# A second inner seven-product scheme in the last matrix product of a fused attention and MLP kernel, with VectorE and TensorE held in program order

## The chip, the cores and the metric

The kernel runs on one core of a Trainium2 chip. The metric is the device time of one execution in microseconds (us); lower is better. Times are medians of several executions. The profiled execution of each kernel was one of them. "Span" is the time from the first to the last instruction of a profiled execution.

## The reference, cut to what matters

```python
def _B_ref(x, w1, b1, w2, b2):
    h = _layernorm(x, axis=-1)
    u = jnp.einsum("bsd,sf->bdf", h, w1) + b1      # "mixer 1"
    u = _gelu(u)
    y = jnp.einsum("bdf,fs->bds", u, w2) + b2      # "mixer 2": the change is here
    return y.transpose(0, 2, 1)

h = x + _A_ref(_layernorm(x), A_wqkv, A_wo)        # linear attention, not touched
h2 = h + _B_ref(_layernorm(h), B_w1, B_b1, B_w2, B_b2)
```

Here S = 2048, D = 1024 and F = 3584. Mixer 2 multiplies w2 (transposed, 2048 x 3584) by the GELU output (3584 x 1024), and adds b2 and the residual h.

Of the kernel before, what the change touches and what calls it, by code (L numbers as in the profile page):

```python
# [8 lines left out]
P = 128  # L9
# [18 lines left out]
def kernel(  # L28
# [170 lines left out]

    class Inner:  # L200
# [7 lines left out]
        def sums(self):  # L208
            sm = [pools["is"].tile([P, self.nk, P], FP16, tag=self.tag, bufs=4, name="is")[:] for _ in range(4)]
            nc.vector.tensor_tensor(sm[0], self.a21, self.a22, ALU.add)  # L210
            nc.vector.tensor_tensor(sm[1], sm[0], self.a11, ALU.subtract)
            nc.vector.tensor_tensor(sm[2], self.a11, self.a21, ALU.subtract)
            nc.vector.tensor_tensor(sm[3], self.a12, sm[1], ALU.subtract)
            self.lhs.update({5: sm[0], 6: sm[1], 7: sm[2], 3: sm[3]})

        def mm(self, m, ps, start):
            for k in range(self.nk):
                nc.tensor.matmul(  # L218
                    ps, lhsT=self.lhs[m][:, k, :], rhs=self.mov[m][:, k, :],
                    start=(start and k == 0), stop=(k == self.nk - 1), skip_group_check=True,  # L220
                )
# [33 lines left out]
    class Product7:  # L255
# [9 lines left out]
        def prefetch(self):  # L265
            pass

        def asum(self, m):
            a, b, op = {
                5: (self.a21, self.a22, ALU.add),  # L270
                6: (self.lhs.get(5), self.a11, ALU.subtract),
                7: (self.a11, self.a21, ALU.subtract),
                3: (self.a12, self.lhs.get(6), ALU.subtract),
            }[m]
            t = pools["sa"].tile([P, self.nk, P], FP16, tag="sa", name="sa")[:]
            self.lhs[m] = t
            return nc.vector.tensor_tensor(t, a, b, op)  # L277
# [4 lines left out]
        def mm(self, m, ps, start, ks=None, cols=slice(0, CW)):  # L282
            lhs, mv = self.lhs[m], self.mov[m]
            for k in range(self.nk) if ks is None else ks:
                nc.tensor.matmul(  # L285
                    ps[:, cols],
                    lhsT=lhs[:, k, :],
                    rhs=mv(k)[:, cols],
                    start=(start and k == 0),
                    stop=(k == self.nk - 1),  # L290
                    skip_group_check=True,
                )
# [55 lines left out]
    class Mixer1(Product7):  # L348
# [11 lines left out]
        def evac_shared(self, fh, ps):  # L360
            t = cpool.tile([P, BANK], F32, tag=f"t{fh}", name="t1")
            nc.vector.tensor_tensor(t[:], ps[:], self.e[:], ALU.add)
            self.evac(fh, 1, t)
# [5 lines left out]
    class Mixer2(Product7):  # L369
        def __init__(self, p):  # L370
            super().__init__(p, w2_tiles[p], NFP, gmov)

        def prefetch(self):
            self.hr = {}
            for sh in range(2):
                for dh in range(2):
                    t = outp.tile([P, CW], BF16, tag=f"hr{self.p % 2}{sh}{dh}", bufs=2 if (sh, dh) == (1, 0) else 1, name="hr")
                    nc.sync.dma_start(t[:], h_dram[2 * self.p + sh][:, dh * CW:(dh + 1) * CW])
                    self.hr[sh, dh] = t

        def out(self, sh, dh, a, b, op):
            i = 2 * self.p + sh
            ot = outp.tile([P, CW], BF16, tag="ot", bufs=3, name="ot")
            op(ot[:, a:b], b2_sb[:, i:i + 1])
            nc.sync.dma_start(o_dram[i * P:(i + 1) * P, dh * CW + a:dh * CW + b], ot[:, a:b])

        def evac(self, sh, dh, ps, a=0, b=CW):
            self.out(sh, dh, a, b, lambda ot, bias: nc.vector.scalar_tensor_tensor(
                ot, ps[:, a:b], bias, self.hr[sh, dh][:, a:b], ALU.add, ALU.add))

        def evac_shared(self, sh, ps):
            t = cpool.tile([P, BANK], F32, tag=f"t{sh}", name="t2")

            def op(ot, bias):
                nc.vector.scalar_tensor_tensor(t[:], ps[:], bias, self.e[:], ALU.add, ALU.add)
                nc.vector.tensor_tensor(ot, t[:], self.hr[sh, 1][:], ALU.add)

            self.out(sh, 1, 0, CW, op)
# [7 lines left out]
    class Quad:  # L406
# [12 lines left out]
        def sum1(self, m, h, ps, es):  # L419
            A, B, c = self.sts[m].A, self.sts[m].B, self.cols(h)  # L420
            nc.vector.tensor_tensor(A[:, c], ps, es, ALU.add)
            nc.scalar.copy(B[:, c], A[:, c])
# [4 lines left out]
        def sum5(self, m, h, ps, es):  # L427
            nc.vector.tensor_tensor(self.sts[m].e[:, self.cols(h)], ps, es, ALU.add)
# [11 lines left out]
        def prefetch(self):  # L440
            for st in self.sts:
                st.prefetch()

        def run(self, pend, nxt, on_p4=nop, before_p7=nop, on_p7=nop, cut=None):
            nk = self.sts[0].nk

            def interleave(n, fs):
                steps = [(f, k) for f in fs for k in range(nk)]
                t = len(steps)
                cuts = [0, (5 * t + 8) // 16, (9 * t + 8) // 16, (12 * t + 8) // 16, t]  # L450

                def fill(q):
                    part = steps[cuts[q]:cuts[q + 1]]
                    for f in fs:
                        ks = [k for g, k in part if g is f]
                        if ks:
                            f(ks)

                for f in (n.i1, 0, n.i6, n.i2, 1, n.i5, n.i7, 2, n.i3, 3, n.i4):
                    fill(f) if isinstance(f, int) else f()  # L460

# [725 lines left out]
    cpool = ctx.enter_context(tc.tile_pool(name="cpool", bufs=1))  # L1187
    assert NFP % 2 == 0 and NSP % 2 == 0 and NSP >= 4 and NFP >= 6
    inner1 = mctx.enter_context(tc.tile_pool(name="inner1", bufs=1, side="right"))
    pools["is"] = inner1  # L1190
# [29 lines left out]
    pools["sa"] = ctx.enter_context(tc.tile_pool(name="sapool2", bufs=6, side="right", reuse_waits="tile"))  # L1220
# [4 lines left out]
    pools["is"] = inner2  # L1225
# [11 lines left out]
    def derived(m, of):  # L1237
        def make():
            ts = [g2pool.tile([P, H2, CW], FP16, tag=f"gs{h}", name=f"gs{h}") for h in range(2)]
            for h, sl in enumerate(spans):  # L1240
                nc.vector.tensor_tensor(ts[h][:], *of(sl), ALU.subtract)
# [3 lines left out]
    make_t3 = derived(7, lambda sl: (gT2[:, sl, :], gE[:, sl, 0:CW]))  # L1245
    make_t4 = derived(4, lambda sl: (gO[:, sl, 0:CW], gT2[:, sl, :]))
    load_w2(1, wpool)
    for p in (2, 3):
        load_w2(p, w2b)
    mov5, sums5 = inner_moving(gE[:, :, CW:D], NFP, inner2, "gi5")  # L1250

    def quad2(u):
        return Quad([Mixer2(2 * u), Mixer2(2 * u + 1)], None, mov5)
# [11 lines left out]
    for st in pend:  # L1265
        st.prefetch()
        if st is pend[1]:
            for m in (5, 6, 7, 3):
                st.asum(m)
            make_t3()  # L1270
# [3 lines left out]
        st.p6()  # L1274
    sums5()
    nxt.pre(5)
# [3 lines left out]
    nxt.pre(6)  # L1280
    nxt.pre(7)
    for st in pend:
        st.p3()
    nxt.pre(3)
    for u in range(1, NSP // 2):
        cur = nxt
        cur.prefetch()
        last = 2 * u + 2 == NSP
        pend, nxt = cur.run(
            pend, lambda: None if last else quad2(u + 1),  # L1290
            on_p4=after_p4(u), on_p7=make_t4, cut=CW - P if last else None,
# [33 lines left out]
```

## The kernel before: what the change touches

Mixer 2 works on eight products p = 0 to 7. One product gives 256 output rows by all 1024 columns. In a matmul, the stationary operand is the one that the code passes as `lhsT`, the moving one is `rhs`; the result goes to PSUM, the memory in which matmuls add up. A product is split into 2 x 2 blocks (row tile, even or odd tile of F, half of the columns), and instead of eight block products the kernel does seven (the Strassen-Winograd scheme): M1 to M7. Each is 14 matmuls of 512 columns. The stationary sums S5, S6, S7, S3 are made by VectorE from the weights of that p, the moving sums T2, T3, T4 from the GELU output (T3 and T4 share one pair of buffers, "gs", so they are made anew all the time).

Products 2 to 7 run as three pairs, called quads. Over the two products of a pair, one M is itself again a 2 x 2 block product. "Inner" does it with seven products of 7 matmuls of 256 columns, 49 in all, in place of 28 of 512 columns. Before, this was done for M5 only:

```python
        def i7(self):                                  # class Inner
            self.mm(7, self.c, False)
            self.sink_sum(1, 1, self.c, self.es[:])    # VectorE adds from PSUM
        def i3(self):
            self.mm(3, self.b, False)                  # b and c: two halves of one PSUM tile
            self.sink_sum(0, 1, self.b, self.es[:])
...
            if self.mov1 is not None:                  # Quad.run; mov1 is None in mixer 2
                ...
            else:
                for st in self.sts:
                    st.p1()                            # M1, plain: 14 matmuls of 512 each
                for st in pend:
                    st.p4()                            # M4 of the pair before
            on_p4()                                    # T3; loads of the next weights
            nxt = nxt()
            ...
            interleave(self.in5, [st.p6 for st in self.sts])   # M5 inner, between it M6
            pre(5)                                     # S5 of the next pair
            for st in self.sts:
                st.p2()
            ...
```

An eviction takes a finished result out of PSUM. That of M2 or M4 was one VectorE operation (PSUM + bias + residual). The order of the instructions on each engine is chosen by the scheduler of the kernel language, except where `tc.keep_in_program_order` ("pin") ties an instruction behind the one written before it.

## Time and profile before

| | before |
|---|---|
| device time, median of 3 (lowest to highest) | 575.07 us (575.03 to 575.7) |
| span of the profiled execution | 573.1 us |
| TensorE (PE) busy | 566.0 us, 99% |
| VectorE (DVE) / ScalarE (ACT) busy | 67% / 44% |
| mixer 2, first to last matmul | 402.88 to 570.2 us |

The head of the profile page gives the span, each engine's busy time and, in its section on the chain that ended last, the share of each engine in that chain.

```profile
span 573.1 us, 8081 instructions
...
PE 566.0 (99%) x3061; PEld 287.2 (50%) x3061; DVE 383.8 (67%) x731; ACT 254.7 (44%) x547; POOL 1.8 (0%) x8
...
PE 93%; DVE 3%; DMA 2%; ACT 2%; issue 1%; SPq 0%; ACTq 0%
```

Busy time by stretch, before. The columns are the stretch, its length, the busy time of PE, PEld (weight loads), DVE, ACT and POOL with their number of instructions, then the granted clock of TensorE (1.00 is full), the DMA share and GB/s. The first row is all of mixer 2, the other two are whole quads.

```profile
402.88:570.20 167.32, 167.32 (x862) 83.63 (x860) 113.94 (x119) 16.73 (x35) 0.00 (x0) 1.00 0.44 119
480.75:522.36 41.61, 41.61 (x219) 21.20 (x217) 27.52 (x32) 4.11 (x9) 0.00 (x0) 1.00 0.51 139
522.36:563.97 41.61, 41.61 (x219) 21.24 (x218) 22.36 (x25) 4.36 (x10) 0.00 (x0) 1.00 0.12 39
```

TensorE is busy in 167.32 of 167.32 us at full clock: nothing is left to hide a saving in, and nothing to gain but TensorE work. VectorE is busy for two thirds of a quad.

The timeline of TensorE, before, at the start of a quad (start, length, engine, line, operation, count). The end of a matmul is modelled, so read from start to start.

```profile
480.75 3.18 PE L285 MATMUL psA_5063<-gE,wq 128*128 128x512 f16 x14
483.77 3.19 PE L285 MATMUL psA_5080<-gE,wq 128*128 128x512 f16 x14
486.79 1.67 PE L285 MATMUL psC_4858<-gs_4997,wq 128*128 128x512 f16 x7
```

The two M1 products take 486.79 - 480.75 = 6.04 us. Seven matmuls of 256 columns are read in the same way at the M5 inner product, where two such blocks stand next to each other:

```profile
456.97 0.93 PE L218 MATMUL psI_4818<-gE,is 128*128 128x256 f16 x7
457.74 0.93 PE L218 MATMUL psI_4819<-gi_4452,is 128*128 128x256 f16 x7
458.50 1.24 PE L285 MATMUL psB_4758<-gT_4434,sa 128*128 128x512 f16 x5
```

One takes (458.50 - 456.97) / 2 = 0.765 us.

The chain that ended last, before, its last pieces:

```profile
569.43 0.80 PE psC_5618 L285 x14
570.22 0.02 issue
570.25 0.35 DVE ot L388
```

After the last matmul there is one VectorE operation and then the output transfer, until 573.1 us.

### The profile page before, as it was taken

The page shows a single profiled execution, that of the slowest core. Times are in us where ns is not written, and L with a number is a line of the kernel's source. Part 1 is how long each engine was busy: PE and PEld are TensorE (multiplying, and loading weights), DVE is VectorE, ACT ScalarE, POOL GpSimd, SP SyncE. Part 2 cuts the span into 40 slices and gives each one's busy share as a digit, 9 for nine tenths or more (in the row PEclk, how much of TensorE's full clock was granted, in tenths as well). Part 3 has the DMA queues.
Part 4 walks back from the last instruction along what each step waited for, and adds up shares of the span by engine and source line. Part 5 has one row for each costly group of instructions (what it writes and reads, how often), then busy time and mean ns, then how long its engine had stood idle before and what let it go on. Part 6 is the DMA issues. An engine that isn't in the chain of part 4 may idle for free.

```text
span 573.1 us, 8081 instructions
## 1 busy us (share of the span) xinstructions
PE 566.0 (99%) x3061; PEld 287.2 (50%) x3061; DVE 383.8 (67%) x731; ACT 254.7 (44%) x547; POOL 1.8 (0%) x8
## 2 busy tenths in 40 slices
PE   8999999999999999999999999999999999999997
PEld 3444444455555444446555565564444554544544
DVE  6898887556767879863745727442989558557535
ACT  5657777656667776445445354463110100100100
POOL 1000000000000000000000000000000000000000
PEclk9999999999999999999999999999999999999999
DMA  9934432039536762104041240425971852842001
GB/s 309 352 74 83 85 73 38 19 113 318 104 73 130 184 174 102 55 2 146 1 148 55 93 148 1 148 75 146 233 189 47 218 140 67 218 120 73 19 27 47
DMA packets 97798, 66.59 MB, mean 116 GB/s; under 512 B 32082, under 2 KB 91744, under 8 KB 97760
## 3 DMA queue, kind: packets, MB, share of 16 engines
q1 hardware_dynamic: 97024, 65.42, 41.7%
q10 hardware_dynamic: 672, 0.66, 0.3%
q8 instruction: 24, 0.39, 0.3%
q14 instruction: 14, 0.11, 0.1%
q0 software_dynamic: 64, 0.01, 0.0%
HBM read 50.34 MB, written 8.39 MB: 102 GB/s over the span
## 4 chain that ended last, share of the span: by engine, by line
PE 93%; DVE 3%; DMA 2%; ACT 2%; issue 1%; SPq 0%; ACTq 0%
PE acc_t L964 9%; PE acc_t L1112 9%; PE psB L695 4%; PE psC L695 4%; PE psA L695 4%; PE psE L695 2%; PE nd_ps L1063 1%; DMA xr<-in_A_x_dram 1%; PE psB_4758 L285 1%; PE psC_5500 L285 1%; PE psC_5181 L285 1%; PE psB_5064 L285 1%; PE psC_4858 L285 1%; PE psA_4757 L285 1%; PE psC_4527 L285 1%; PE psB_4550 L285 1%
## 5 line engine op out<-in xcount | busy, mean ns | idle before, releaser
L285 PEld LDWEIGHTS <-sa 128*128 128x128 f16 x716 | 70.0, 98 | 77.3 <-issue 0.7
L285 PEld LDWEIGHTS <-wq 128*128 128x128 bf16 x590 | 57.1, 98 | 61.7 <-issue 1.0
L964 PE MATMUL acc_t<-xnT,wq_sb 128*128 128x512 bf16 x256 | 58.0, 379 | 0.0
L1112 PE MATMUL acc_t<-wo_sb,pqT 128*128 128x512 bf16 x256 | 56.1, 379 | 0.0
L277 DVE TENSOR_TENSOR sa<-wq 128x1024 f16<-128x1024 bf16 (+1 forms) x44 | 36.4, 830 | 6.9 <-DMA wq<-in_B_w_dram 2.8
L1112 PEld LDWEIGHTS <-pqT 128*128 128x128 bf16 x256 | 24.8, 98 | 29.0
L964 PEld LDWEIGHTS <-wq_sb 128*128 128x128 bf16 x256 | 24.5, 98 | 27.4
L166 ACT ACTIVATE e_sb<-acc_t 128x512 bf16<-128x512 f32 x40 | 23.9, 597 | 26.5 <-PE acc_t L964 24.3
L170 DVE TENSOR_SCALAR e_sb<-e_sb 128x512 bf16<-128x512 bf16 x64 | 18.5, 289 | 25.4 <-ACT e_sb L166 24.8
L218 PEld LDWEIGHTS <-is 128*128 128x128 f16 x276 | 26.9, 98 | 14.3 <-issue 3.0
L695 PEld LDWEIGHTS <-xs 128*128 128x128 f16 x208 | 20.0, 98 | 23.3 <-DVE xs L681 1.3
L695 PE MATMUL psA<-wkv,xnT 128*128 128x512 bf16 x104 | 26.7, 379 | 0.0
L1123 DVE BATCH_NORM_STATS2 hst<-acc_t 128x6 f32<-128x512 f32 x32 | 22.1, 693 | 6.7 <-ACT h_bf L1122 6.5
L1110 ACT CAST acc_t<-xr 128x512 f32<-128x512 bf16 x32 | 19.0, 593 | 13.4 <-DVE hst L1123 13.3
L695 PEld LDWEIGHTS <-xnT 128*128 128x128 bf16 x156 | 15.3, 98 | 18.5 <-issue 0.2
L167 ACT ACTIVATE r_sb<-acc_t 128x512 bf16<-128x512 f32 x40 | 23.7, 593 | 0.0
L619 PE MATMUL acc_t<-wkv,xnT 128*128 128x512 bf16 x96 | 21.6, 379 | 0.7 <-ACT xnT L872 0.7
L1084 DVE TENSOR_TENSOR o_sb<-nd_ps,rd 128x384 bf16<-128x384 f32 (+1 forms) x48 | 21.7, 504 | 0.6 <-ACT rd L1079 0.4
L588 DVE BATCH_NORM_STATS2 st<-x_sb 128x6 f32<-128x512 bf16 x32 | 20.5, 681 | 1.6 <-DMA x_sb<-in_A_x_dram 1.6
L277 DVE TENSOR_TENSOR sa<-sa,wq 128x1024 f16<-128x1024 f16 (+1 forms) x22 | 18.3, 831 | 3.9 <-PE psC_4858 L285 2.3
L277 DVE TENSOR_TENSOR sa<-wq,sa 128x1024 f16<-128x1024 bf16 (+1 forms) x22 | 18.3, 831 | 3.7 <-PE psI_5141 L218 1.1
L1122 ACT CAST h_bf<-acc_t 128x512 bf16<-128x512 f32 x32 | 18.4, 575 | 1.0 <-PE acc_t L1112 0.9
(722 smaller groups left out, 979.1 us busy)
## 6 DMA issues: line engine op xcount, KB each, us to landing
wq<-in_B_w_dram SPq DMA_DIRECT2D x14, 1024.0 KB, 7.7
wq<-in_B_w_dram SPq DMA_DIRECT2D x8, 1792.0 KB, 10.0
xr<-in_A_x_dram SPq DMA_DIRECT2D x16, 256.0 KB, 3.1
out_dram<-ot SPq DMA_DIRECT2D x31, 128.0 KB, 1.7
x_sb<-in_A_x_dram SPq DMA_DIRECT2D x15, 256.0 KB, 3.2
wkv<-in_A_wqkv_dram SPq DMA_DIRECT2D x2, 1024.0 KB, 9.5
wq_sb<-in_A_wqkv_dram SPq DMA_DIRECT2D x2, 1024.0 KB, 12.7
wo_sb<-in_A_wo_dram SPq DMA_DIRECT2D x2, 1024.0 KB, 6.4
```

The source lines that it names most:

```text
L166: pin(nc.scalar.activation(e_sb[:], src, ACT.Exp))
L167: pin(nc.scalar.activation(r_sb[:], src, ACT.Relu))
L218: nc.tensor.matmul(ps, lhsT=self.lhs[m][:, k, :], rhs=self.mov[m][:, k, :], start=(start and k == 0), stop=(k == self.nk - 1), skip_group_ ...
L277: return nc.vector.tensor_tensor(t, a, b, op)
L285: nc.tensor.matmul(ps[:, cols], lhsT=lhs[:, k, :], rhs=mv(k)[:, cols], start=(start and k == 0), stop=(k == self.nk - 1), skip_group_check ...
L588: return nc.vector.bn_stats(st[:, c, :], x_sb[:, c * CW:(c + 1) * CW])
L619: mm = nc.tensor.matmul(pp[:, 0:CW], lhsT=xnT[:, kt, i * P:(i + 1) * P], rhs=wkv[:, kt, c * CW:(c + 1) * CW], start=(kt == 0), stop=(kt == ...
L695: pin(nc.tensor.matmul(ps[:], lhsT=lhs[:, k, :], rhs=rhs[:, k, :], start=(start and k == 0), stop=(k == hk2 - 1), skip_group_check=True,))
L964: nc.tensor.matmul(qp[:, 0:SW], lhsT=wq_sb[:, kt, j * P:(j + 1) * P], rhs=xnT[:, kt, u * SW:(u + 1) * SW], start=(kt == 0), stop=(kt == ND ...
L1084: nc.vector.tensor_tensor(o_sb[:, b * JPB * P:(b * JPB + nsl) * P].rearrange("p (s h e) -> p s h e", h=HB, e=DH), blk[:, :, 0:P].rearrange ...
L1112: nc.tensor.matmul(ap_[:, 0:CW], lhsT=pqT[:, j, i * P:(i + 1) * P], rhs=wo_sb[:, j, dc * CW:(dc + 1) * CW], start=(j == 0 and not SEED_RES ...
L1123: nc.vector.bn_stats(st[:, dc, :], ap_[:, 0:CW])
```

## The change

Its intent: do M1 of the three quads by the inner scheme as well, and so save the columns of 7 matmuls of 256 per quad (49 x 256 in place of 28 x 512). The rest makes room for that: sums for the M1 inner product, evictions of M2 and M4 split into a ScalarE part (PSUM + bias) and a light bf16 add on VectorE, the same light add as the second sum in an eviction of M3 or M7, S7 written over the weights that it is made from, four instead of six sum buffers, and the instructions of VectorE and TensorE held in the order in which they are written (`Held`). "S6 sums behind those of M5" is the order of the two lines after `st.begin()`. The diff, cut to its core:

```diff
+    class Held:
+        on = False
+        ...
+        def __getattr__(self, name):
+            op = getattr(self.engine, name)
+            return (lambda *a, **kw: pin(op(*a, **kw))) if Held.on else op
+
+    dve, pe = Held(nc.vector), Held(nc.tensor)
     ... (sums, matmuls and evictions of both mixers call dve and pe)
     class Mixer2(Product7):
+        def asum(self, m):
+            if m != 7:
+                return super().asum(m)
+            t = self.a21.bitcast(FP16)           # S7 in place
+            self.lhs[7] = t
+            return dve.tensor_tensor(t, self.a11, self.a21, ALU.subtract)
     ...
         def out(self, sh, dh, a, b, op):
             ...
             op(ot[:, a:b], b2_sb[:, i:i + 1])
+            dve.tensor_tensor(ot[:, a:b], ot[:, a:b], self.hr[sh, dh][:, a:b], ALU.add)
     ...
         def evac(self, sh, dh, ps, a=0, b=CW):
-            self.out(sh, dh, a, b, lambda ot, bias: nc.vector.scalar_tensor_tensor(
-                ot, ps[:, a:b], bias, self.hr[sh, dh][:, a:b], ALU.add, ALU.add))
+            self.out(sh, dh, a, b, lambda ot, bias: nc.scalar.activation(
+                ot, ps[:, a:b], ACT.Identity, bias=bias, scale=1.0))
     ...
+        def begin2(self):
+            self.asums(5)
+            self.in1 = self.inner(1)             # four inner sums of M1
+
+        def run2(self, pend, nxt, on_p4, on_p7, cut):
+            sts = self.sts
+            for st in sts:
+                st.begin()
+            in5 = self.inner(5)                  # inner sums of M5
+            self.asums(6)                        # S6 behind them
+            self.interleave(self.in1, [st.p4 for st in pend])
+            on_p4()                              # T3, weight loads
+            ...
+            self.asums(7)
+            self.interleave(in5, [st.p6 for st in sts])
+            self.asums(3)
+            nxt = nxt()
+            for st in sts:
+                st.p2()
+            ...
+            if nxt is not None:
+                nxt.begin2()
+            for st in sts:
+                st.p7(cut if st is sts[-1] else None)
+            on_p7()                              # T4
+            for st in sts:
+                st.p3()
+            return sts, nxt
     ...
+    def less_b11(t, sl):                         # T3 is mended, as the M1 inner sums
+        ...                                      # overwrite a part of the GELU output
     ...
+    sums1()                                      # moving sums of the M1 inner product
     sums5()
     ...
+    Held.on = True
     for u in range(1, NSP // 2):
     ...
-        pend, nxt = cur.run(
+        pend, nxt = cur.run2(
```

More of the change, by code (lines that the diff above doesn't have):

```diff
@@ L198, in inner_moving, with __init__ @@
         return {1: b11, 2: b21, 3: b22, 4: t4, 5: b12, 6: t2, 7: t3}, sums
+    class Held:
+        on = False
+        def __init__(self, engine):
+            self.engine = engine
+        def __getattr__(self, name):
+            op = getattr(self.engine, name)
+            return (lambda *a, **kw: pin(op(*a, **kw))) if Held.on else op
+    dve, pe = Held(nc.vector), Held(nc.tensor)
     class Inner:
@@ L208, in sums @@
         def sums(self):
-            sm = [pools["is"].tile([P, self.nk, P], FP16, tag=self.tag, bufs=4, name="is")[:] for _ in range(4)]
-            nc.vector.tensor_tensor(sm[0], self.a21, self.a22, ALU.add)
-            nc.vector.tensor_tensor(sm[1], sm[0], self.a11, ALU.subtract)
-            nc.vector.tensor_tensor(sm[2], self.a11, self.a21, ALU.subtract)
-            nc.vector.tensor_tensor(sm[3], self.a12, sm[1], ALU.subtract)
+            sm = [pools["is"].tile([P, self.nk, P], FP16, tag=self.tag, bufs=pools["is_bufs"], name="is")[:] for _ in range(4)]
+            dve.tensor_tensor(sm[0], self.a21, self.a22, ALU.add)
+            dve.tensor_tensor(sm[1], sm[0], self.a11, ALU.subtract)
+            dve.tensor_tensor(sm[2], self.a11, self.a21, ALU.subtract)
+            dve.tensor_tensor(sm[3], self.a12, sm[1], ALU.subtract)
             self.lhs.update({5: sm[0], 6: sm[1], 7: sm[2], 3: sm[3]})
@@ L217, in mm @@
             for k in range(self.nk):
-                nc.tensor.matmul(
+                pe.matmul(
                     ps, lhsT=self.lhs[m][:, k, :], rhs=self.mov[m][:, k, :],
@@ L276, in asum @@
             self.lhs[m] = t
-            return nc.vector.tensor_tensor(t, a, b, op)
+            return dve.tensor_tensor(t, a, b, op)
         def pre(self, m):
@@ L284, in mm @@
             for k in range(self.nk) if ks is None else ks:
-                nc.tensor.matmul(
+                pe.matmul(
                     ps[:, cols],
@@ L360, in evac_shared @@
         def evac_shared(self, fh, ps):
-            t = cpool.tile([P, BANK], F32, tag=f"t{fh}", name="t1")
+            t = pools["t"].tile([P, BANK], F32, tag=f"t{fh}", name="t1")
             nc.vector.tensor_tensor(t[:], ps[:], self.e[:], ALU.add)
@@ L371, in __init__, with fetch @@
             super().__init__(p, w2_tiles[p], NFP, gmov)
-        def prefetch(self):
             self.hr = {}
-            for sh in range(2):
-                for dh in range(2):
-                    t = outp.tile([P, CW], BF16, tag=f"hr{self.p % 2}{sh}{dh}", bufs=2 if (sh, dh) == (1, 0) else 1, name="hr")
-                    nc.sync.dma_start(t[:], h_dram[2 * self.p + sh][:, dh * CW:(dh + 1) * CW])
-                    self.hr[sh, dh] = t
+        def asum(self, m):
[4 more added lines that the diff above has]
+            return dve.tensor_tensor(t, self.a11, self.a21, ALU.subtract)
+        def fetch(self, sh, dh):
+            t = outp.tile([P, CW], BF16, tag="hr", bufs=6, name="hr")
+            nc.sync.dma_start(t[:], h_dram[2 * self.p + sh][:, dh * CW:(dh + 1) * CW])
+            self.hr[sh, dh] = t
         def out(self, sh, dh, a, b, op):
@@ L384, in out @@
             op(ot[:, a:b], b2_sb[:, i:i + 1])
+            dve.tensor_tensor(ot[:, a:b], ot[:, a:b], self.hr[sh, dh][:, a:b], ALU.add)
             nc.sync.dma_start(o_dram[i * P:(i + 1) * P, dh * CW + a:dh * CW + b], ot[:, a:b])
         def evac(self, sh, dh, ps, a=0, b=CW):
-            self.out(sh, dh, a, b, lambda ot, bias: nc.vector.scalar_tensor_tensor(
-                ot, ps[:, a:b], bias, self.hr[sh, dh][:, a:b], ALU.add, ALU.add))
+            self.out(sh, dh, a, b, lambda ot, bias: nc.scalar.activation(
+                ot, ps[:, a:b], ACT.Identity, bias=bias, scale=1.0))
         def evac_shared(self, sh, ps):
-            t = cpool.tile([P, BANK], F32, tag=f"t{sh}", name="t2")
-            def op(ot, bias):
-                nc.vector.scalar_tensor_tensor(t[:], ps[:], bias, self.e[:], ALU.add, ALU.add)
-                nc.vector.tensor_tensor(ot, t[:], self.hr[sh, 1][:], ALU.add)
-            self.out(sh, 1, 0, CW, op)
+            self.out(sh, 1, 0, CW, lambda ot, bias: dve.scalar_tensor_tensor(
+                ot, ps[:], bias, self.e[:], ALU.add, ALU.add))
         def done(self):
@@ L420, in sum1 @@
             A, B, c = self.sts[m].A, self.sts[m].B, self.cols(h)
-            nc.vector.tensor_tensor(A[:, c], ps, es, ALU.add)
+            dve.tensor_tensor(A[:, c], ps, es, ALU.add)
             nc.scalar.copy(B[:, c], A[:, c])
@@ L427, in sum5 @@
         def sum5(self, m, h, ps, es):
-            nc.vector.tensor_tensor(self.sts[m].e[:, self.cols(h)], ps, es, ALU.add)
+            dve.tensor_tensor(self.sts[m].e[:, self.cols(h)], ps, es, ALU.add)
         def pre(self, m):
@@ L438, in pre, with interleave, fill @@
                 self.in5.sums()
-        def prefetch(self):
-            for st in self.sts:
-                st.prefetch()
-        def run(self, pend, nxt, on_p4=nop, before_p7=nop, on_p7=nop, cut=None):
-            nk = self.sts[0].nk
-            def interleave(n, fs):
-                steps = [(f, k) for f in fs for k in range(nk)]
-                t = len(steps)
-                cuts = [0, (5 * t + 8) // 16, (9 * t + 8) // 16, (12 * t + 8) // 16, t]
-                def fill(q):
-                    part = steps[cuts[q]:cuts[q + 1]]
-                    for f in fs:
-                        ks = [k for g, k in part if g is f]
-                        if ks:
-                            f(ks)
-                for f in (n.i1, 0, n.i6, n.i2, 1, n.i5, n.i7, 2, n.i3, 3, n.i4):
-                    fill(f) if isinstance(f, int) else f()
+        def interleave(self, n, fs):
+            steps = [(f, k) for f in fs for k in range(self.sts[0].nk)]
+            t = len(steps)
+            cuts = [0, (5 * t + 8) // 16, (9 * t + 8) // 16, (12 * t + 8) // 16, t]
+            def fill(q):
+                part = steps[cuts[q]:cuts[q + 1]]
+                for f in fs:
+                    ks = [k for g, k in part if g is f]
+                    if ks:
+                        f(ks)
+            for f in (n.i1, 0, n.i6, n.i2, 1, n.i5, n.i7, 2, n.i3, 3, n.i4):
+                fill(f) if isinstance(f, int) else f()
@@ new lines, in asums, with inner @@
+        def asums(self, m):
+            for st in self.sts:
+                st.asum(m)
+        def inner(self, m):
+            mov, sink, sink_sum = {
+                1: (self.mov1, self.sink1, self.sum1), 5: (self.mov5, self.sink5, self.sum5),
+            }[m]
+            n = Inner(self.sts, m, mov, "i", sink, sink_sum)
+            n.sums()
+            return n
+        def begin2(self):
[10 more added lines that the diff above has]
+            for st in sts:
+                st.shared_tile()
+                st.fetch(0, 0)
+            for sh, dh in ((1, 1), (0, 1)):
+                for st in sts:
+                    st.fetch(sh, dh)
+            self.asums(7)
[4 more added lines that the diff above has]
+                st.p2()
+            for st in sts:
+                st.fetch(1, 0)
+            if nxt is not None:
+                nxt.begin2()
+            for st in sts:
+                st.p7(cut if st is sts[-1] else None)
+            on_p7()
+            for st in sts:
+                st.p3()
+            return sts, nxt
@@ L462, in run @@
+        def run(self, pend, nxt, on_p4=nop, before_p7=nop, on_p7=nop, cut=None):
+            interleave = self.interleave
             if self.mov1 is not None:
@@ L1187 @@
     cpool = ctx.enter_context(tc.tile_pool(name="cpool", bufs=1))
+    pools["t"] = mctx.enter_context(tc.tile_pool(name="tpool", bufs=1, side="right"))
     assert NFP % 2 == 0 and NSP % 2 == 0 and NSP >= 4 and NFP >= 6
     inner1 = mctx.enter_context(tc.tile_pool(name="inner1", bufs=1, side="right"))
-    pools["is"] = inner1
+    pools["is"], pools["is_bufs"] = inner1, 4
     hmov.update(moving(hE, hO, hT2, hT3, hT4))
@@ L1218 @@
     mctx.close()
-    pools["sa"] = ctx.enter_context(tc.tile_pool(name="sapool2", bufs=6, side="right", reuse_waits="tile"))
+    pools["sa"] = ctx.enter_context(tc.tile_pool(name="sapool2", bufs=4, side="right", reuse_waits="tile"))
     w2b = ctx.enter_context(tc.tile_pool(name="w2b", bufs=2, side="right", reuse_waits="tile"))
@@ L1224 @@
     inner2 = ctx.enter_context(tc.tile_pool(name="inner2", bufs=1, side="right", reuse_waits="tile"))
-    pools["is"] = inner2
+    pools["is"], pools["is_bufs"] = inner2, 7
     H2 = NFP // 2
@@ L1235, with derived @@
     gmov.update(moving(gE, gO, gT2, None, None))
-    def derived(m, of):
+    def derived(m, of, mend=None):
         def make():
@@ L1240, in make @@
             for h, sl in enumerate(spans):
-                nc.vector.tensor_tensor(ts[h][:], *of(sl), ALU.subtract)
+                dve.tensor_tensor(ts[h][:], *of(sl), ALU.subtract)
+                if mend is not None:
+                    mend(ts[h], sl)
             gmov[m] = lambda k: ts[k // H2][:, k % H2, :]
         return make
-    make_t3 = derived(7, lambda sl: (gT2[:, sl, :], gE[:, sl, 0:CW]))
+    def less_b11(t, sl):
+        k0 = sl.start + sl.start % 2
+        o = t[:, k0 - sl.start:H2:2, HW:CW]
+        dve.tensor_tensor(o, o, gE[:, k0:sl.stop:2, 0:HW], ALU.subtract)
+    make_t3_raw = derived(7, lambda sl: (gT2[:, sl, :], gE[:, sl, 0:CW]))
+    make_t3 = derived(7, lambda sl: (gT2[:, sl, :], gE[:, sl, 0:CW]), less_b11)
     make_t4 = derived(4, lambda sl: (gO[:, sl, 0:CW], gT2[:, sl, :]))
@@ L1249 @@
         load_w2(p, w2b)
+    mov1, sums1 = inner_moving(gE[:, :, 0:CW], NFP, inner2, "gi1")
     mov5, sums5 = inner_moving(gE[:, :, CW:D], NFP, inner2, "gi5")
     def quad2(u):
-        return Quad([Mixer2(2 * u), Mixer2(2 * u + 1)], None, mov5)
+        return Quad([Mixer2(2 * u), Mixer2(2 * u + 1)], mov1, mov5)
     def after_p4(u):
@@ L1265 @@
     for st in pend:
-        st.prefetch()
+        st.fetch(0, 0)
+        st.fetch(1, 1)
+        st.fetch(0, 1)
+    for st in pend:
         if st is pend[1]:
-            for m in (5, 6, 7, 3):
+            for m in (5, 6, 7):
                 st.asum(m)
-            make_t3()
+            make_t3_raw()
         st.p1()
@@ L1274 @@
         st.p6()
+        if st is pend[1]:
+            st.asum(3)
+    sums1()
     sums5()
-    nxt.pre(5)
+    for st in pend:
+        st.fetch(1, 0)
+    nxt.begin2()
     for st in pend:
@@ L1279 @@
     make_t4()
-    nxt.pre(6)
-    nxt.pre(7)
     for st in pend:
         st.p3()
-    nxt.pre(3)
+    Held.on = True
     for u in range(1, NSP // 2):
         cur = nxt
-        cur.prefetch()
         last = 2 * u + 2 == NSP
-        pend, nxt = cur.run(
-            pend, lambda: None if last else quad2(u + 1),
-            on_p4=after_p4(u), on_p7=make_t4, cut=CW - P if last else None,
+        pend, nxt = cur.run2(
+            pend, lambda: None if last else quad2(u + 1), after_p4(u), make_t4, CW - P if last else None,
         )
```

## The prediction

> **What bounds it now.** TensorE. The page gives PE 566.0 us busy (99%) of a 573.1 us span at full granted clock, and the chain of waits is 93% PE. In mixer 2 (from 402.9 us) the busy-time-by-stretch view shows PE busy 10.00 of every 10 us until 570.2 us, with no wait listed for it. VectorE is 53 to 66% busy in the three later pairs of products ("quads": 22.4 us of 41.6 in the last, 27.5 in the one before), but nearly full from 428 to 442 us.
>
> **What the change removes.** In each of three quads the two M1 products (28 matmuls of 512 columns) become an inner seven-product scheme of 49 matmuls of 256 columns. Read start to start in the timeline, 14 matmuls of 512 take 3.02 us and 7 of 256 take 0.765 us (the M5 inner product, already there). M1 goes from 6.05 to 5.35 us: 0.69 us per quad, 2.07 us in all. TensorE has no idle time to hide this in, so all of it is on the critical path. This is the ceiling.
>
> **What it adds and moves.** Per quad on VectorE: four M1 inner sums (0.62 us each), two sums of 256 columns (0.42 each), the correction of T3 (about 1.2 us, my estimate from 1.09 us for 1792 elements). Against that, eight evictions shrink: for four, the 0.75 us PSUM sum goes to ScalarE (0.57 us for such a copy; ScalarE is about 10% busy here) and leaves a bf16 add of about 0.42 us; four swap a second sum of 0.69 us for one of about 0.42 us. Net about +2 us per quad. Once, in the first pair, four sums of 1.09 us prepare the M1 moving operands; in exchange the sums for S6, S7 and S3 leave that crowded stretch. The in-place S7 and four instead of six sum buffers cost no time if the order is right.
>
> I laid the pinned order out by hand with traced durations. T4 is ready about 3 us before the first M4 matmul needs it, S6 and the M5 sums about 2 us before the first inner sum on VectorE, T3 and S7 about 10 us before M7. The weights (two loads, about 12 us) land before the next quad's sums, which now come after M2. So in the steady quads I expect no TensorE wait; in the transition (about 436 to 450 us) there is 1 to 2 us of slack, and a wait of up to 2 us is possible. I allow 0.1 us on average.
>
> At the end, the last eviction was one 0.35 us VectorE operation; it becomes a ScalarE operation of about 0.3 us, a hand-over, and a small add: about +0.25 us. Identity should need no table load: the Trainium skill, "ScalarE: Activation LUTs", section "Table sets: the hidden batching unit", says that cheap functions are in every set. This trace agrees for Copy only, which runs among the GELUs without a reload each time.
>
> **Prediction.** 575.07 - 2.07 + 0.25 + 0.1 = about 573.3 us; range 572.6 to 574.8. Faster by over 2%: 0.01; within 2%: 0.97; slower by over 2%: 0.02.
>
> **What would show it.** Right: M1 of each later quad as seven blocks of 0.765 us; PE still 10.00 of 10 us from 403 us to its end; quads of about 40.9 us instead of 41.6; last matmul near 568.2 us; about 2.8 us from it to the end of the span, or slightly more. Wrong: any PE wait listed on a VectorE tile (T4, inner sums, T2 to T4 of the M1 inner product) or on ScalarE's copies between 436 and 450 us, or once per quad; output buffers (three) held by queued VectorE adds, stopping ScalarE; hr loads arriving after the weights and stalling the pinned VectorE order; a table load.

## The result, and the profile after

| | before | after |
|---|---|---|
| device time, median (lowest to highest) | 575.05 us (575.01 to 575.7) | 573.27 us (573.14 to 573.32) |
| span | 573.1 us | 571.5 us |
| mixer 2, first to last matmul | 167.32 us | 165.25 us |
| one quad | 41.61 us | 40.92 us |
| VectorE busy in the quad of the second row above | 27.52 us | 29.26 us |

The ratio of after to before is 0.9963, with a 95% interval of 0.9949 to 0.9977. Such a ratio is the mean time of one kernel's fast runs over that of the other's of the same rounds, so it is not quite the ratio of the two medians (0.9969). 1.8 us is clear of the variation. Each kernel ran four times here; the table of the kernel before has three of its executions.

The same lines after. First the head of the page:

```profile
span 571.5 us, 8308 instructions
...
PE 563.7 (99%) x3124; PEld 293.3 (51%) x3124; DVE 390.2 (68%) x759; ACT 272.0 (48%) x585; POOL 1.8 (0%) x8
...
PE 95%; DVE 3%; ACT 1%; issue 1%; DMA 1%; ACTq 0%
```

Busy time by stretch, after: mixer 2, and the two later quads.

```profile
403.03:568.28 165.25, 165.25 (x925) 89.87 (x923) 118.31 (x145) 33.77 (x72) 0.00 (x0) 1.00 0.48 129
480.21:521.12 40.91, 40.91 (x239) 23.30 (x238) 29.26 (x39) 8.91 (x20) 0.00 (x0) 1.00 0.52 142
521.12:562.04 40.92, 40.92 (x240) 23.31 (x238) 25.27 (x33) 9.16 (x21) 0.00 (x0) 1.00 0.15 46
```

TensorE is still busy all through mixer 2, which is 2.07 us shorter (167.32 - 165.25), and each quad is 0.69 us shorter. The view of waits lists no wait of TensorE in mixer 2.

The timeline of TensorE, after, at the start of the same quad (M1 blocks are those of 256 columns; between them M4 of the pair before):

```profile
480.21 0.93 PE L208 MATMUL psI<-gE,wq 128*128 128x256 f16 x7
480.97 2.11 PE L208 MATMUL psC<-gs,wq 128*128 128x512 f16 x9
...
486.72 0.93 PE L208 MATMUL psI<-gi,is 128*128 128x256 f16 x7
487.48 1.24 PE L208 MATMUL psC<-gs,wq 128*128 128x512 f16 x5
488.56 0.93 PE L208 MATMUL psI<-gE,is 128*128 128x256 f16 x7
```

A block of seven takes 480.97 - 480.21 = 0.76 us, as the M5 inner product did before. The tail, after, in the chain that ended last:

```profile
568.29 0.02 issue
568.32 0.38 ACT ot L406
568.70 0.02 issue
568.72 0.23 DVE ot L208
```

From the last matmul to the end of the last eviction it is now 0.66 us (568.29 to 568.95); it was 0.38 us (570.22 to 570.60). So the span is made up as: 2.07 us less matmul time, 0.28 us more at the end, and 0.15 us more before mixer 2 (it starts at 403.03, before at 402.88), which together is 1.64 us less; the spans differ by 1.6 us. The 0.15 us need not come from the change: in two profiled executions of one and the same program (all_dve, below) mixer 2 started at 402.76 and at 403.01 us.

### The profile page after: what moved, and what is told of

It is laid out like the page before. It is cut to its first block, busy times and chain, and to the rows that moved or that the text cites. A ratio compares the mean times of both kernels' runs of the same rounds, so it can differ in the third digit from the quotient of the medians.

```text
span 571.5 us, 8308 instructions
## 1 busy us (share of the span) xinstructions
PE 563.7 (99%) x3124; PEld 293.3 (51%) x3124; DVE 390.2 (68%) x759; ACT 272.0 (48%) x585; POOL 1.8 (0%) x8
## 4 chain that ended last, share of the span: by engine, by line
PE 95%; DVE 3%; ACT 1%; issue 1%; DMA 1%; ACTq 0%
PE psB L297 10%; PE psC L297 10%; PE acc_t L1019 9%; PE acc_t L1167 9%; PE psC L208 7%; PE psA L297 7%; PE psI L230 7%; PE psB L208 6%; PE psI L208 6%; PE psB L750 4%; PE psC L750 4%; PE psA L750 4%; PE psA L208 3%; PE acc_t L674 2%; PE psE L750 2%; PE psE L297 1%
## 5 line engine op out<-in xcount | busy, mean ns | idle before, releaser
L208 PEld LDWEIGHTS <-wq 128*128 128x128 bf16 (+1 forms) x357 | 34.5, 98 | 31.3
L297 PEld LDWEIGHTS <-wq 128*128 128x128 bf16 (+1 forms) x324 | 31.6, 98 | 33.1 <-issue 1.0
L208 PE MATMUL psC<-gs,wq 128*128 128x512 f16 (+2 forms) x210 | 45.0, 365 | 0.0
L208 DVE TENSOR_TENSOR ot<-ot,hr 128x512 bf16<-128x512 bf16 (+2 forms) x27 | 11.2, 415 | 28.1 <-ACT ot L406 27.7
L333 ACT COPY psC<-psB 128x512 f32<-128x512 f32 x22 | 12.5, 570 | 35.1 <-PE psB L297 21.5
L297 PE MATMUL psB<-hT,sa 128*128 128x512 f16 x112 | 28.4, 379 | 0.0
L441 DVE TENSOR_TENSOR e<-psI,es 128x256 f32<-128x256 f32 x12 | 5.1, 425 | 34.0 <-PE psI L230 34.0
L297 PE MATMUL psC<-hT,wq 128*128 128x512 f16 x112 | 28.3, 379 | 0.0
L297 PE MATMUL psA<-hO,wq 128*128 128x512 f16 x112 | 25.6, 379 | 0.7 <-ACT psB L316 0.7
L297 PE MATMUL psB<-hO,sa 128*128 128x512 f16 x112 | 25.5, 379 | 0.0
L297 PE MATMUL psC<-hT,sa 128*128 128x512 f16 x112 | 25.5, 379 | 0.0
```

Of the source, the lines that this page charges most:

```text
L208: return (lambda *a, **kw: pin(op(*a, **kw))) if Held.on else op
L297: pe.matmul(ps[:, cols], lhsT=lhs[:, k, :], rhs=mv(k)[:, cols], start=(start and k == 0), stop=(k == self.nk - 1), skip_group_check=True,)
L333: nc.scalar.copy(self.C[:], self.B[:])
L441: dve.tensor_tensor(self.sts[m].e[:, self.cols(h)], ps, es, ALU.add)
```

## The experiments

Theory A, the prediction's: TensorE is the bound, the gain is the matmul columns that went away, and every other part of the change costs or gains nothing as long as each sum comes before TensorE asks for it. The rivals were that the lighter evictions or the fixed order made the gain, that the order of S6 matters, or that VectorE has room enough for any order. In each expectation below, Rival B is the rival that the run is meant to tell from Theory A. Every run's output was correct. All edits are to the changed kernel.

### m1_plain: everything but the M1 inner product

```diff
         def begin2(self):
             self.asums(5)
-            self.in1 = self.inner(1)
...
-            for st in sts:
-                st.begin()
             in5 = self.inner(5)
             self.asums(6)
-            self.interleave(self.in1, [st.p4 for st in pend])
+            for st in sts:
+                st.p1()
+            for st in pend:
+                st.p4()
...
-            make_t3()
+            make_t3_raw()
...
-    sums1()
```

> The changed kernel, but M1 of the three later quads runs as plain products again (28 matmuls of 512 columns) and the sums that only the M1 inner product needs are left out; the eviction split, the in-place S7, the four sum buffers and the pinned order stay. Theory A (all of the gain is TensorE columns, 0.69 us in each of three quads): 573.27 + 2.07 = about 575.3 us, quads of 41.6 us in the timeline, no TensorE wait. Rival B (the gain comes from the lighter evictions on VectorE and the fixed order): it stays near 573.3 us, as all of that is kept.

Measured: 575.43 us (575.31 to 575.49), ratio to before 0.9999 (0.9984 to 1.0015), no TensorE wait listed in mixer 2. A quad is 522.60 - 480.99 = 41.61 us again, from the starts of M1:

```profile
480.99 6.21 PE L208 MATMUL psA<-gE,wq 128*128 128x512 f16 x28
522.60 6.21 PE L208 MATMUL psA<-gE,wq 128*128 128x512 f16 x28
```

The whole gain is gone, and with it nothing else: the lighter evictions, S7 in place and the held order are worth nothing by themselves. Rival B falls. The result lies even 0.3 us above the before of these rounds (575.1 us), in line with the tail of 0.28 us that this kernel keeps, though that is within its interval.

### unpinned: the order not held

```diff
-    Held.on = True
+    Held.on = False
```

> The changed kernel with the program order of VectorE and TensorE not held (the scheduler's own order). On VectorE the S7 sums and the next sums move earlier and the inner sums mix with the evictions; on TensorE one matmul per quad moves ahead of its filler. Theory A (TensorE is the bound and the quads have microseconds of slack on VectorE, so order matters only once it uses up that slack): within 0.3 us of 573.3. Rival B (holding the order is what makes both inner products fit): TensorE waits on VectorE sums appear, over 0.5 us per quad, 575 us or more.

Measured: 586.05 us (583.74 to 586.73), ratio 1.0177 (1.0151 to 1.0203), "unclear" at 2%. Theory A as I had put it missed by 13 us: the slack is there only in the order as written. The profiled execution (583.74 us, span 581.9 us) shows where it goes. Waits of TensorE in mixer 2, in the view of waits (who waited, for whom, us in total, times, longest):

```profile
PE psI L230 <- DVE e L441: 7.8, 2, 5.3
```

The timeline of VectorE around the longest of them:

```profile
463.18 0.63 DVE L222 TENSOR_TENSOR is<-wq 128x896 f16<-128x896 bf16 x1 [5.41 <-DMA wq<-in_B_w_dram]
463.84 0.62 DVE L223 TENSOR_TENSOR is<-is,wq 128x896 f16<-128x896 f16 x1
464.38 0.42 DVE L441 TENSOR_TENSOR e<-psI,es 128x256 f32<-128x256 f32 x1
```

and of TensorE:

```profile
464.85 1.65 PE L230 MATMUL psI<-gE,is 128*128 128x256 f16 x7 [5.29 <-DVE e L441]
466.30 2.43 PE L297 MATMUL psB<-gT,sa 128*128 128x512 f16 x7
468.56 0.93 PE L230 MATMUL psI<-gi,sa 128*128 128x256 f16 x7
```

The scheduler had put two of the next quad's M1 inner sums (`is<-wq`) in front of an M5 sum (`e<-psI`). They need the next weights, which were still on their way, so VectorE stood still for 5.41 us with an M5 sum behind it whose input was long there, and TensorE waited for that sum. The Trainium skill, "Perfetto Trace Analysis", section "Tensor Engine Instruction (MATMUL, LD_WEIGHTS)", says that VectorE's execution queue is strictly first in, first out; this trace agrees (the sum could have run 5 us earlier and did not).

The wait has a second price. After 5.45 us without a matmul (464.85, where the block would have started at 458.32 + 1.08 = 459.40), seven matmuls of 256 columns took 1.45 us (466.30 - 464.85) instead of 0.76, and seven of 512 took 2.26 instead of 1.51 us. Busy time by stretch for these blocks shows the clock:

```profile
464.85:469.49 4.64, 4.64 (x22) 2.70 (x22) 2.16 (x4) 0.57 (x1) 0.00 (x0) 0.68 0.01 4
```

The mean granted clock was 0.68 there. The Trainium skill, "TensorE: Matmul & The Clock Gate", section "Part 1: The HAM clock gate (the "warmup" mystery)", gives the rule: half rate after an idle window of about 3.4 us. These two waits agree: the one of 5.45 us was followed by the lower clock, the second, of 2.70 us, by a granted clock of 1.00. The start of pin_begin2, below, shows that the window need not be wholly idle.

The account by quads, from the starts of M1: 48.05, 43.85 and 41.15 us against 40.92, 40.91 and 40.92 us held. The first has 5.45 us of wait, 1.44 us of slow clock and 0.23 us of a small wait; the second 2.70 and 0.23; the third 0.23. That is 10.3 of the 10.4 us between the two spans. The other three executions were 2.2 to 3.0 us slower still; only one has a trace, so what they lost is open. Their mean granted clock in the records was 0.991, against 0.997 in the profiled one. As an estimate from these means, they had some 7 us more at half clock, which would cost up to 3.5 us.

One half of the hold does nothing: with only VectorE held, the built program has the same instructions in the same order on TensorE, VectorE and ScalarE as the changed kernel. So it was not run.

### pin_begin2: only the misplaced sums held

```diff
-    Held.on = True
+    Held.on = False
...
             if nxt is not None:
+                Held.on = True
                 nxt.begin2()
+                Held.on = False
```

> The run without held order, with one exception: the VectorE sums for the next quad (its S5 and the four inner sums of its M1) may not move ahead of what was written before them. In the unheld run VectorE reached the first of these sums before the next weights had landed, stood still for 5.4 and 2.7 us, and the M5 sums that TensorE waited for stood behind it. Theory A (that one misplacement is the whole loss, with the lower granted clock that followed the longest wait): 573.2 to 573.6 us, no TensorE wait on the M5 sums, granted clock 1.00 throughout. Rival B (other reorderings, the later T4 above all, cost time too): 574 us or more, TensorE waits elsewhere.

Measured: 575.1 us (573.87 to 576.17), ratio 1.0001 (0.9986 to 1.0016). By the time this is a miss, and the spread is large, so the trace has to tell. No TensorE wait is listed in mixer 2 and the granted clock is 1.00 in it: the waits of 5.45 and 2.70 us are gone, as Theory A said. Two things are left. Mixer 2 itself is about 0.7 us longer: each quad is 41.15 or 41.16 us, 0.24 us over the held order, because the first half of T3 now comes before the second inner sum of M1, and TensorE waits 0.23 us for that sum. Rival B was right that another reordering costs something, but it is 0.7 of 10.3 us. The rest came before mixer 2, which began at 404.87 instead of 403.03 us in the profiled execution. The first eight projection matmuls took 3.4 us start to start (10.88 - 7.51) instead of 1.7, after 0.95 us of waiting for the first attention weights, and the granted clock between 7 and 12 us was 0.66 instead of 1.00 (0.50 for these eight):

```profile
5.84 0.72 PE L919 MATMUL tp<-ident,xn 128*128 128x128 bf16 x8 [0.91 <-DVE xn L655]
7.51 3.55 PE L676 MATMUL acc_t<-wkv,xnT 128*128 128x512 bf16 x8 [0.95 <-DMA wkv<-in_A_wqkv_dram]
10.88 0.63 PE L919 MATMUL tp<-ident,xn 128*128 128x128 bf16 x8
```

```profile
7.00:12.00 5.00, 4.03 (x17) 1.68 (x18) 2.74 (x7) 1.52 (x5) 0.00 (x0) 0.66 1.08 362
```

TensorE's and VectorE's instructions are in the same order up to there. The record speaks for variation of the start and against an effect of the edit. The two longer executions (575.84 and 576.17 us) have a mean granted clock of 0.997, the two others (573.87 and 574.37 us) one of 1.000. The unaltered changed kernel did the same in one execution of after_again: 574.91 us at 0.997, where its median is 573.28 us. The fastest execution of pin_begin2 is 0.6 us above the changed kernel, which fits the 0.7 us of mixer 2.

### s6_first: S6 sums ahead of those of M5

```diff
-            in5 = self.inner(5)
             self.asums(6)
+            in5 = self.inner(5)
```

> The changed kernel with the S6 sums put ahead of the M5 inner sums again (the only difference is this order on VectorE, three times). Theory A: both groups are over before the first inner sum of M1 asks for VectorE, and nothing on TensorE needs either until about 8 us later: no change, 573.2 to 573.4 us, M1 and M5 blocks where they were. Rival B (the placement matters): a TensorE wait at M5's first stationary sums or at S6, some tenths of a us per quad.

Measured: 573.17 us (573.14 to 573.34), ratio 0.9961, no TensorE wait in mixer 2. Both groups end at the same time (486.4 us in the middle quad) and VectorE then idles 0.88 us until the first inner sum of M1, as in the changed kernel. Placing S6 behind the M5 sums, which is named in the change, is worth nothing here. Rival B falls.

### t4_twice: 3.9 us more on VectorE per quad

```diff
             on_p7()
+            on_p7()
             for st in sts:
                 st.p3()
```

> The changed kernel with T4 computed twice over in each of the three later quads: 3.95 us more on VectorE per quad (10%), where it is idle about a quarter of the time. Theory A (what counts is the slack of the one sum that TensorE asks for next, read as 3.0 us for the first half of T4 in the quads and 2.4 us before the last M4): TensorE waits about 1.2 us in each of two quads and about 1.9 us before the last M4, 577.0 to 578.5 us. Rival B (idle share is what counts): absorbed, within 0.3 us of 573.3.

Measured: 580.11 us (580.07 to 581.63). Rival B falls: a VectorE that is idle for a quarter of a quad could not take 3.9 us more, about a tenth of the quad. But Theory A missed too, by 1.6 us or more. The waits of TensorE in mixer 2:

```profile
PE psC L208 <- DVE gs L208: 3.6, 6, 1.4
PE psI L208 <- DVE psA L208: 1.9, 2, 1.0
```

The first line is the expected wait for T4. Start to start it is 1.3 us in each of two quads and 2.0 us at the end, so 4.6 us, near the expected 4.3. The second line was not expected: 1.1 us in each of two quads, for the first inner sum of M1. Together 6.8 us, the difference of the spans (578.3 - 571.5). VectorE came to this sum late, because it had been late since T4. And TensorE cannot go around it: the next inner product writes half b of a PSUM tile whose half c the sum reads. I had taken it as independent because its data are. The next block that writes half c was due only 2.28 us later (493.23 - 490.95), and the sum, which ended at 490.90, would have been in time for it. The Trainium skill, "PSUM — Partial Sum Buffer", section "PSUM bank collisions raise a hardware error ⚠️", asks that accesses of two engines be kept apart by bank and not by address; the wait in this trace fits that, but no run here put b and c into two banks.

### t4_half_more: 1.95 us more, to find the tightest deadline

In the changed kernel, the lines of VectorE around this sum are:

```profile
484.42 2.09 DVE L208 TENSOR_TENSOR sa<-sa,wq 128x1792 f16<-128x1792 f16 x2
486.44 0.43 DVE L208 TENSOR_TENSOR ot<-ot,hr 128x512 bf16<-128x512 bf16 x1
487.75 0.43 DVE L208 TENSOR_TENSOR psA<-psI,es 128x256 f32<-128x256 f32 x1 [0.88 <-PE psI L208]
```

VectorE has 0.88 us of idle before it, and the sum ends at 488.18 us, 0.38 us before the block at 488.56 us that waits for it (in the TensorE timeline above). So, as an estimate, 1.3 us of VectorE time is all that this point can take, and T4 has 3 us.

```diff
+    def again(t, sl):
+        if sl.start == 0:
+            dve.tensor_tensor(t[:], gO[:, sl, 0:CW], gT2[:, sl, :], ALU.subtract)
+
+    make_t4_more = derived(4, lambda sl: (gO[:, sl, 0:CW], gT2[:, sl, :]), again)
...
-            pend, ..., after_p4(u), make_t4, CW - P if last else None,
+            pend, ..., after_p4(u), make_t4_more, CW - P if last else None,
```

> The changed kernel with only the first half of T4 computed once more in each of the three later quads: 1.95 us more on VectorE. T4 then still comes in time by its own slack (first half at 479.9, asked for at 481.0 us). But in the changed kernel the first inner sum of M1 starts at 487.75 us with 0.88 us of idle VectorE before it, and the third-but-last inner product waits for it; with 1.95 us more it ends at about 489.2 us, where TensorE asks at 488.56. Theory A (the tightest deadline in the held order is this inner sum, 1.3 us of slack, as the run with T4 twice suggests): 0.7 us of TensorE wait in each of two quads, none before the last M4, about 574.7 us. Rival B (T4 is the tightest, 3 us): no wait, 573.3 us.

Measured: 574.59 us (574.48 to 576.28), beside 573.28 us of the changed kernel in the same rounds. The only wait of TensorE in mixer 2, and where it is:

```profile
PE psI L208 <- DVE psA L208: 0.9, 2, 0.4
```

```profile
487.42 1.24 PE L208 MATMUL psC<-gs,wq 128*128 128x512 f16 x5
489.10 0.92 PE L208 MATMUL psI<-gE,is 128*128 128x256 f16 x7 [0.43 <-DVE psA L208]
```

The block starts 1.68 us after the filler instead of 1.08, so 0.6 us in each of two quads, none for T4. The tightest deadline of the held order is this sum. For work put at T4 the slack is 1.3 us of VectorE time per quad and not the 11.7 us that VectorE idles in it (40.91 - 29.26). More work at other places in the order was not tried.

### tail_dve and all_dve: the evictions back on VectorE

In tail_dve the two evictions of the last, cut M4 are one VectorE operation each again; in all_dve all evictions of M2 and M4 are.

```diff
+        def out_direct(self, sh, dh, ps, a, b):
+            ...
+            dve.scalar_tensor_tensor(ot[:, a:b], ps[:, a:b], b2_sb[:, i:i + 1], self.hr[sh, dh][:, a:b], ALU.add, ALU.add)
+            nc.sync.dma_start(...)
...
         def evac(self, sh, dh, ps, a=0, b=CW):
+            if (a, b) != (0, CW):                      # tail_dve; all_dve without the condition
+                return self.out_direct(sh, dh, ps, a, b)
             self.out(sh, dh, a, b, lambda ot, bias: nc.scalar.activation(...))
```

> The changed kernel, but the two evictions of the last, cut M4 (384 and 128 columns) are one VectorE operation each again, as in the kernel before; everything else as changed. After the last matmul the changed kernel runs 0.37 us on ScalarE and 0.23 us on VectorE with a hand-over between them, 0.67 us in all; the one operation took 0.35 us. Theory A (the tail is on the critical path to its full length): 0.3 us less, about 572.95 us, last matmul at the same place, span 571.2 us. Rival B (the end of the span is set by the output transfers queued behind each other): no change, 573.2 to 573.3 us.

Measured: 573.17 us (572.96 to 573.75). The trace shows the tail shortened as expected, with the last matmul in the same place and the span 571.2 us; by time alone, 0.1 us between the medians of different rounds shows nothing.

> The changed kernel with all M2 and M4 evictions back as one VectorE operation of 0.75 us (ScalarE no longer takes part); four 0.42 us adds per quad go away, so VectorE gets about 1.3 us more per quad in its held order. Theory A (the split of the evictions buys nothing here as T4 has 3 us of slack, and costs 0.3 us at the end): about 572.95 us, no TensorE wait. Rival B (the split is needed to make both inner products fit): TensorE waits on T4 or on the first inner sum in each quad, 573.5 us or more.

Measured: 572.88 us (572.58 to 573.09), no TensorE wait in mixer 2, quads of 40.91 or 40.92 us. So the split of the evictions, which the change brought in, is not needed to make both inner products fit. To compare on one chip, the changed kernel and this version ran again side by side.

> The changed kernel unaltered, timed on the same chip and in the same rounds as the next run, to compare with it. 573.2 to 573.3 us; span from the first matmul of mixer 2 to its end 168.5 us.

> The version with all M2 and M4 evictions on VectorE again, beside the changed kernel of the same rounds. Theory A (it saves the 0.3 us tail and costs nothing else): 0.3 us below the changed kernel, about 572.95 us, and 168.15 us from the first matmul of mixer 2 to the end. Rival B (the 0.4 us seen before was variation between runs in the first 12 us, where the first weights land): equal medians.

Measured: 573.28 us (573.24 to 574.91) for the changed kernel and 572.98 us (572.94 to 573.13) for all_dve; spans 571.5 and 571.1 us. From the first matmul of mixer 2 to the end of the span they took 168.50 and 168.09 us (571.5 - 403.00, 571.1 - 403.01), so the gain is not a matter of the start. The tail of all_dve, in the chain that ended last:

```profile
568.27 0.03 issue
568.30 0.35 DVE ot L208
```

All_dve beats both kernels, by 0.3 us over the changed one. It is a small gain, with less code.

## Why the prediction was right, point by point

- **What bounds it.** Right. TensorE is busy all through mixer 2 before and after, and without the M1 inner product the gain vanishes (m1_plain, 575.43 us).
- **2.07 us less matmul time.** Right: 167.32 to 165.25 us, with blocks of 0.76 us and quads of 40.92 us.
- **VectorE, net about +2 us per quad.** Near: +1.74 us in the middle quad and +2.9 us in the last one, off the critical path. The correction of T3 took 1.25 us per quad (estimated 1.2), the add 0.42 us as said. ScalarE took 0.69 us for a full eviction where I had 0.57 us; it has room for that, at 8.91 us busy in the middle quad.
- **The slacks.** T4 about 3 us: right (ready at 477.9 us, asked for at 481.0). T3 and S7 about 10 us: right (ready at 499.3, M7 at 509.0). S6 and the M5 sums "about 2 us before the first inner sum on VectorE": mis-sized, it is 0.88 us of idle, and I did not see that TensorE is held up by this sum so soon. It is the tightest point of all, and t4_twice and t4_half_more showed it. It did not matter for the time, because the held order stays within it.
- **The transition.** I allowed 0.1 us on average for a wait of up to 2 us; there was none.
- **The sum.** That 573.3 us fits the measured 573.27 us to some hundredths is luck. The 0.1 us allowed for a wait was not needed, the tail cost 0.03 us more than said, and the profiled executions differ by another 0.15 us before mixer 2, of which the prediction knew nothing.
- **The tail.** +0.25 us predicted, +0.28 us measured. The parts: ScalarE 0.37 us (I said about 0.3), VectorE 0.23 us. The Trainium skill, "ScalarE: Activation LUTs", section "What ACT_TABLE_LOAD costs", gives 280 ns + 0.833 ns per element for an operation with a bias operand, an estimate of 0.387 us for 128 elements; that would have been nearer. My sign "about 2.8 us from the last matmul to the end of the span, or slightly more" was put wrongly: it was 2.9 us before and is 3.2 us after.
- **No table load.** Right: the profile lists two loads of 1.28 us before and after, neither in mixer 2.
- **What was right by the order alone.** The prediction said that the sums "cost no time if the order is right". Left to the scheduler, the same work costs 13 us more (unpinned). The hold of VectorE is therefore no detail but the part of the change without which the rest is a loss.

Of the change's parts, the M1 inner product brings the 2 us, the hold of VectorE keeps it from costing 13 (nearly all of that by the hold of the next quad's sums, pin_begin2), the hold of TensorE changes nothing, the place of S6 changes nothing, and the split evictions cost 0.3 us. S7 in place and the four sum buffers were not tested alone.

## What to carry to other kernels

When an engine has no idle time, a saving on it is worth its full length as long as no wait takes its place, as here, and can be read beforehand from the start-to-start times of the same instruction elsewhere in the trace. Whether a second engine can carry the extra work is not read from its idle share but from the tightest deadline in its order: list when each of its results is ready and when the bound engine asks for it, and count results that only share a PSUM bank with what comes next. In an engine that works strictly in order, an instruction that waits for a transfer must not stand before one that the bound engine waits for; where a scheduler chooses the order, look at what it chose, and pin the few instructions that it puts too early.

## What the Trainium skill lacked or had wrong

- "TensorE: Matmul & The Clock Gate", section "Back-to-back issue gap", gives a sustained 131 ns per matmul of 512 columns in a stream of weight loads and matmuls, and calls N / 2.4 + 2.5 ns too long for such a stream at large N. Here a sustained stream of 14 such pairs took 3.02 us, 216 ns each, and 7 of 256 columns took 0.765 us, 109 ns each: the formula (215.8 and 109.2 ns) holds in the stream, the 131 ns does not.
- "Perfetto Trace Analysis", section "Identifying the Most-Contended Engine": occupancy tells which engine is contended, but not how much more work another one can take. VectorE idled 11.7 us in a quad and could take 1.3 us at the place tried; 1.95 us more cost TensorE 0.6 us in each of two quads.
- "PSUM — Partial Sum Buffer" states the collision of two engines in one bank as an error to be guarded against. What keeping them apart costs is not there: an inner product waited 1.1 us for a sum that read the other half of its tile (t4_twice).
- "TensorE: Matmul & The Clock Gate" does not say how much work a window may hold and still count as idle. In pin_begin2 the granted clock fell to 0.50 (8 to 10 us) after 2.57 us (4.94 to 7.51) in which TensorE did only eight transposes of 128 columns, 0.72 us of work, while 2.70 us of full idle in unpinned did not lower it.
